# Splitting four output stores at the end of a convolution-and-MLP kernel into halves of 64 rows

## The chip, the cores and the metric

The kernel runs on one core of a Trainium2 chip. The metric is the device time of one execution in microseconds (us); lower is better. Each quoted time of a kernel is the median of several executions.

## The reference

The input is `x` with 8 sequences of 4096 positions and 192 features. Each position is replaced by a weighted sum of itself and the six positions before it (zeros ahead of the start); the seven weights are a softmax, one set for each of eight groups of 24 features. The 32768 resulting rows go through a two-layer perceptron with a leaky ReLU:

```
out[b,s,f] = sum_k softmax(weight)[head(f), k] * x_pad[b, s+k, f]
h = out.reshape(B*S, 192) @ w_in        # 192 -> 2048
g = maximum(0.01*h, h)
result = g @ w_out                      # 2048 -> 192, float32, 32768 rows
```

## The kernel before

**Tiling.** Two sequences are handled side by side, one on partitions 0 to 63 and the other on 64 to 127 (the index `e`), and a block is 512 positions of such a pair. There are 32 blocks. The first two are cut into two groups of 256 positions each, so that the main loop (L654) runs over 34 groups.

**Work in a group.** VectorE computes the convolution of the next group (L226, L232). TensorE multiplies by `w_in` (`mm1`, L494), ScalarE applies the leaky ReLU while it moves the product from PSUM to the tile `g` (L501), and TensorE multiplies an earlier group's `g` by `w_out`. In most of the program this second product is computed transposed (`mm2_slot`, L574); VectorE turns it back (`evac_t`, L596) into the tile `o_t`, and four DMAs on SP's queue (L610) store it, each reading 32 partitions.

**The end.** The last block has no later group to hide behind. Its second product is computed untransposed, in eight pieces of 128 rows (L715 to L719), which I call p0 to p7. In the code they have the numbers `LAST` to `LAST + 7`, where `LAST` is 16. For each piece TensorE runs 16 matmuls of 128x192 (`mm2_one`, L511) into a PSUM tile `po`, and then `evac_o` (L615) is called:

- VectorE copies the `po` tile to an SBUF tile `o_sb` (L622). For these pieces every call takes a new tile (L618, L619).
- SP issues one DMA that stores the 128 rows of 192 floats (L625). That is 96 KB.

**What orders the end.** The pool of `o_sb` tiles has four buffers (L66), so the copies of p4 to p7 write the buffers of p0 to p3 and wait until those stores have landed. The PSUM pool has four buffers too (L68), so the matmuls of p4 wait for the copy of p0, and so on. The program is laid out by hand (L70): SP takes its DMAs in the order of the code. So the stores of p0 to p7 stand behind the four `o_t` stores of the group before.

**Completion semaphores.** The built program gives SP's DMAs eight completion semaphores in rotation. Each DMA waits, before SP issues it, for the DMA that used the same semaphore eight places earlier. I call these semaphores lanes. At the end of the kernel before, the four `o_t` stores of the next-to-last group have lanes 0 to 3, p0 to p3 have lanes 4 to 7, and p4 to p7 have lanes 0 to 3 again.

Of the kernel before, what the change touches and what calls it, by code (L numbers as in the profile page):

```python
# [15 lines left out]
def kernel(  # L16
# [8 lines left out]
    nc = tc.nc  # L25
# [46 lines left out]
    out_rows = out.rearrange("(r s) d -> r s d", r=B)  # L72
# [226 lines left out]
    for sign, off in ((1, 0), (-1, GRP - 1)):  # L299
        nc.gpsimd.affine_select(  # L300
            out=sel[:, :, 0, :], in_=sel[:, :, 0, :], compare_op=mybir.AluOpType.is_ge,
# [42 lines left out]
    for h in range(2):  # L344
        cs = slice(h * NFC // (2 * RUN), (h + 1) * NFC // (2 * RUN))
        nc.gpsimd.dma_start(
            out=w_out.rearrange("p (c i) d -> p c i d", i=RUN)[:, cs],
            in_=moe_w_out.rearrange("(c p i) d -> p c i d", p=128, i=RUN)[:, cs],
# [7 lines left out]
    def warm(n, cols=HT):  # L356
# [10 lines left out]
        out=nmax, in_=w9[:, 0:K], axis=mybir.AxisListType.X,  # L367
# [3 lines left out]
        out=w9[:, 0:K], in_=w9[:, 0:K], func=mybir.ActivationFunctionType.Exp,  # L371
# [61 lines left out]
    for p in range(2):  # L433
# [10 lines left out]
        out=rsum, in0=wml[:, :, K:], scalar=1e-9, in1=whm[:, :, 0, K:],  # L444
# [34 lines left out]
    LAST = len(subs)  # L479
# [39 lines left out]
    def mm2_row_slot(q):  # L519

        p, fc = divmod(q, 2 * NFC)
        rnd, fc = divmod(fc, NFC)
        pair = (2 * p, 2 * p + 1)
        first, last = fc == 0, fc == NFC - 1
        if first and rnd == 0:
            for n in pair:
                po[n] = psum_o.tile([128, D], FP32, name="po", tag="po")
        for rt in range(2):  # L530
            ins = mm2_one(
                rt, pair[rt ^ rnd], fc, first and rnd == 0, last and rnd == 1
            )
            if first and rnd == 1:
                sync(ins, seal, "both row tiles have left these banks")
        if last and rnd == 0:
            seal_round(p, ins)
        if last and rnd == 1:
            evac_o(pair[0])

    def seal_round(p, ins):


        nonlocal seal
        if p == 0:
            seal = nc.scalar.copy(out=junk, in_=junk)
        else:
            seal = evac_o(2 * p - 1)
        sync(seal, ins, "between the rounds")
# [65 lines left out]
    def evac_o(n):  # L615
        b, e, s = subs[n]
        rp, st = divmod(b, NB)
        if n % 2 == 0 or n >= LAST:  # L618
            osb[n] = o_pool.tile([128, 2, D], FP32, name="o_sb")  # L619
        o_sb = osb[n if n >= LAST else n - n % 2]  # L620
        copy = nc.scalar.copy if b < NHALF else nc.vector.tensor_copy
        ins = copy(out=o_sb[:, n % 2, :], in_=po.pop(n))  # L622
        if n >= LAST:
            t0 = st * ST + s * 128
            nc.sync.dma_start(out=out_rows[2 * rp + e, t0 : t0 + 128, :], in_=o_sb[:, n % 2, :])  # L625
        elif n % 2 == 1:
            t0 = st * ST + (s - 1) * 128
            nc.sync.dma_start(
                out=out_rows[2 * rp + e, t0 : t0 + 256, :].rearrange("(c p) d -> p c d", p=128),
                in_=o_sb,  # L630
            )
        return ins
# [21 lines left out]
    for i, grp in enumerate(groups):  # L654
        blk, t0, T = grp
# [10 lines left out]
        for j in range(steps):  # L666
# [41 lines left out]
            if i == NSW and j == steps - 1:  # L708
                evac_o(LAST - 1)
                slot = NSW * NR * NFC  # L710
# [39 lines left out]
```

## Time and profile before

| what | us |
|---|---|
| median of 4 executions | 681.55 |
| their range | 681.27 to 681.7 |
| the profiled execution, whole time | 681.7 |
| its span, first to last instruction | 680.0 |
| outside the span (681.7 - 680.0) | 1.7 |
| TensorE busy | 675.8 |

The profile is of one execution. Its times count from the start of the span. "SPq" rows are DMAs as SP issues them: the duration of such a row is the time that SP is held, not the time in which the data move. The time from issue to landing is given apart, and ends when the completion is seen. A chain of waits follows the work that ended last back to what released it.

### The profile page before, as it was taken

What the parts mean: (1) busy time and instruction counts of PE and PEld (TensorE: products, weight loads), DVE (VectorE), ACT (ScalarE), POOL (GpSimd) and SP (SyncE); (2) the same over time, 40 slices, a digit from 0 to 9 for tenths busy, and PEclk for the clock granted to TensorE, in tenths of its full rate; (3) what the DMA queues carried; (4) which work ended last, traced back from release to release, by engine and by line L of the source; (5) the groups of instructions that cost most, each with busy time, mean ns of one, the idle gap of its engine ahead of it and who ended that gap; (6) DMA issues with size and microseconds to landing.
All of it is one profiled execution on the core that took longest, in us unless ns stands there. A gap on an engine that the chain in (4) does not pass through costs nothing.

```text
span 680.0 us, 27088 instructions
## 1 busy us (share of the span) xinstructions
PE 675.8 (99%) x12444; PEld 447.3 (66%) x12444; DVE 481.5 (71%) x811; ACT 518.7 (76%) x608; POOL 146.3 (22%) x205
## 2 busy tenths in 40 slices
PE   9999999999999999999999999999999999999998
PEld 6997666666666666666666666666666666666667
DVE  7989468766768666778667687667786676876612
ACT  7899777777777778777777877778777777777781
POOL 7455210222201222211222112222022220000000
PEclk9999999999999999999999999999999999999999
DMA  9799846666647557556557476565575573321123
GB/s 153 91 111 110 57 80 88 80 64 73 91 76 96 71 56 89 81 87 86 64 65 94 75 95 77 56 83 83 84 91 66 59 96 71 72 56 35 32 50 94
DMA packets 213826, 53.27 MB, mean 78 GB/s; under 512 B 209232, under 2 KB 213328, under 8 KB 213712
## 3 DMA queue, kind: packets, MB, share of 16 engines
q0 software_dynamic: 98752, 13.97, 30.2%
q1 hardware_dynamic: 114944, 37.57, 27.8%
q8 instruction: 97, 1.59, 0.9%
q14 instruction: 17, 0.14, 0.1%
q10 hardware_dynamic: 16, 0.00, 0.0%
HBM read 28.31 MB, written 25.17 MB: 79 GB/s over the span
## 4 chain that ended last, share of the span: by engine, by line
PE 99%; ACT 0%; DVE 0%; issue 0%
PE ph L494 49%; PE acc L574 44%; PE po L511 5%; PE acc L257 1%; PE warm L358 0%; PE ptr L188 0%; ACT xt L199 0%; PE ptr L179 0%; DVE o_sb L622 0%; PE wps L394 0%
## 5 line engine op out<-in xcount | busy, mean ns | idle before, releaser
L501 ACT ACTIVATE g<-ph 128x1024 bf16<-128x1024 f32 x512 | 496.6, 1021 | 140.5 <-PE ph L494 140.3
L232 DVE SCALAR_TENSOR_TENSOR yt<-xt,wk,yt 128x512 bf16<-128x512 bf16 (+1 forms) x582 | 381.3, 727 | 0.2
L494 PE MATMUL ph<-yt,w_in 64*64 64x512 bf16 (+2 forms) x6048 | 377.1, 369 | 0.0
L574 PE MATMUL acc<-g,w_out 64*64 64x512 bf16 x5568 | 339.9, 376 | 0.0
L494 PEld LDWEIGHTS <-w_in 64*64 64x64 bf16 (+1 forms) x6048 | 229.1, 131 | 103.1 <-issue 0.8
L574 PEld LDWEIGHTS <-w_out 64*64 64x64 bf16 x5568 | 178.6, 118 | 118.7
L99 POOL DMA_DIRECT2D x_bf<-in_x_dram x180 | 133.9, 774 | 409.1 <-DMA xt<-x_bf 407.2
L596 DVE STREAM_TRANSPOSE o_t<-acc 128x512 f32<-128x512 f32 x87 | 73.3, 883 | 181.6 <-PE acc L574 181.6
L511 PE MATMUL po<-w_out,g 64*128 64x192 bf16 (+1 forms) x640 | 36.8, 243 | 0.0
L511 PEld LDWEIGHTS <-g 64*128 64x128 bf16 (+1 forms) x640 | 32.6, 95 | 3.2 <-issue 0.4
L226 DVE TENSOR_SCALAR yt<-xt,wk 128x512 bf16<-128x512 bf16 (+1 forms) x97 | 29.2, 328 | 3.2 <-DMA xt<-x_bf 3.0
L584 ACT COPY junk<-junk 128x1 f32<-128x1 f32 x58 | 11.1, 192 | 4.1
L622 DVE COPY o_sb<-po 128x192 f32<-128x192 f32 x8 | 2.8, 357 | 6.8 <-PE po L511 3.8
L257 PE MATMUL acc<-xt,diag 64*64 64x256 bf16 x140 | 5.4, 272 | 0.2 <-ACT xt L199 0.2
L622 ACT COPY o_sb<-po 128x192 f32<-128x192 f32 x16 | 5.1, 324 | 0.3
L257 PEld LDWEIGHTS <-diag 64*64 64x64 bf16 x140 | 4.4, 106 | 1.2 <-issue 0.7
L358 PE MATMUL warm<-const-bfloat16-1.0 128*128 128x512 bf16 (+3 forms) x12 | 3.9, 477 | 0.8 <-PEq L734 0.8
L152 POOL DMA_DIRECT2D x_half<-in_x_dram x6 | 4.2, 714 | 1.2 <-DMA w_in<-in_moe_w_in_dram 1.2
L358 PEld LDWEIGHTS <-const-bfloat16-1.0 128*128 128x128 bf16 x12 | 1.5, 135 | 2.5 <-issue 2.5
L148 POOL DMA_DIRECT2D x_rows<-in_x_dram x4 | 2.9, 742 | 0.0
L413 DVE TENSOR_TENSOR diag<-ident,whm 128x448 bf16<-128x448 bf16 (+1 forms) x5 | 2.6, 581 | 0.0
L421 ACT ACTIVATE diag<-ident,whm 128x64 bf16<-128x64 bf16 x10 | 2.5, 337 | 0.0
(47 smaller groups left out, 24.6 us busy)
## 6 DMA issues: line engine op xcount, KB each, us to landing
out_dram<-o_t SPq DMA_DIRECT2D x116, 192.0 KB, 4.6
x_bf<-in_x_dram POOLq DMA_DIRECT2D x180, 64.0 KB, 3.1
out_dram<-o_sb SPq DMA_DIRECT2D x8, 192.0 KB, 3.2
xt<-x_bf SPq DMA_TRANSPOSE x90, 3.9
w_out<-in_moe_w_out_dram POOLq DMA_DIRECT2D x2, 384.0 KB, 7.9
out_dram<-o_sb SPq DMA_DIRECT2D x8, 96.0 KB, 2.0
w_in<-in_moe_w_in_dram POOLq DMA_DIRECT2D x2, 256.0 KB, 5.3
x_nat<-in_x_dram SPq DMA_DIRECT2D x2, 192.0 KB, 2.7
```

What stands on the lines that cost most here:

```text
L99: ins = nc.gpsimd.dma_start(out=t[:, c, :, e, :], in_=src[2 * rp + e, :, :, c * CH : (c + 1) * CH],)
L226: lambda s=src, d=dst, c=c: nc.vector.tensor_scalar_mul(d, s, wk[:, c, 0:1])
L232: lambda s=src, d=dst, c=c, k=k: nc.vector.scalar_tensor_tensor(out=d, in0=s, scalar=wk[:, c, k : k + 1], in1=d, op0=mybir.AluOpType.mult, ...
L257: lambda k=k, p=p, a=a, ps=ps, to=to, acc=accs[e * apart]: nc.tensor.matmul(out=acc[to, :T], lhsT=diag[c][ps, p, k, :], rhs=xt[0][ps, c, a ...
L358: nc.tensor.matmul(out=wa[:, 0, 0:cols], lhsT=ones[:, 0:128], rhs=ones[:, 0:cols], start=True, stop=True,)
L494: nc.tensor.matmul(out=ph[m : m + M, e, i * T : (i + 1) * T], lhsT=w_in_of(f, e, c, m, m + M), rhs=y[ps, c, t0 : t0 + T], start=(c == chun ...
L501: act = nc.scalar.activation(out=g[blk][:, nf * u : nf * (u + 1), :, t0 : t0 + T], in_=ph.rearrange("p e (i t) -> p i e t", i=nf), func=my ...
L511: return nc.tensor.matmul(out=po[m], lhsT=g[b][ps, fc, e, s * 128 : (s + 1) * 128], rhs=w_out[ps, fc, :], start=start, stop=stop,)
L574: ins = nc.tensor.matmul(out=acc2[gi, r][e * CH : (e + 1) * CH, 0:T], lhsT=w_out_of(ps, fc, r), rhs=g[b][ps, fc, e, t0 : t0 + T], start=fi ...
L584: seal = nc.scalar.copy(out=junk, in_=junk)
L596: nc.vector.transpose(out=osb[gi, 0][:, 0 : T // GB, :, r], in_=acc2.pop((gi, r))[:, 0:T].rearrange("p (j k) -> p j k", k=GB),)
L622: ins = copy(out=o_sb[:, n % 2, :], in_=po.pop(n))
```

## The change

The stores of p0 to p3 become two DMAs each, one for rows 0 to 63 and one for rows 64 to 127. The stores of p4 to p7 remain one DMA each; this includes the last one. Nothing else differs: the instructions of the four compute engines keep their order, and SP issues 12 DMAs where it issued 8.

```diff
         if n >= LAST:
             t0 = st * ST + s * 128
-            nc.sync.dma_start(out=out_rows[2 * rp + e, t0 : t0 + 128, :], in_=o_sb[:, n % 2, :])
+            parts = 2 if n < LAST + 4 else 1
+            for h in range(parts):
+                ps = slice(h * 128 // parts, (h + 1) * 128 // parts)
+                nc.sync.dma_start(
+                    out=out_rows[2 * rp + e, t0 + ps.start : t0 + ps.stop, :],
+                    in_=o_sb[ps, n % 2, :],
+                )
```

With four more DMAs the lanes move on. The halves of p0 and p1 take lanes 4, 5, 6 and 7, the halves of p2 take 0 and 1, those of p3 take 2 and 3, and p4 to p7 take 4 to 7.

## The prediction, made before the changed kernel ran

> **What bounds the kernel now.** I read the chain of waits first, for the last 20 us. Columns: start, duration, what.
>
> ```profile
> 666.14 10.68 PE po L511 x128
> 676.82 0.02 issue
> 676.85 0.36 DVE o_sb L622
> ```
>
> TensorE runs the eight pieces without a gap until 676.82, and VectorE's copy of p7 follows at once. After 677.21 (676.85 + 0.36) only the store of p7 and its landing remain. So the change, which touches no TensorE work, can act on this tail alone: it must delay the copy or the store of p7 to cost anything, and cannot end TensorE earlier.
>
> Next, VectorE in order of time. A bracket gives the idle time before an instruction and what ended it.
>
> ```profile
> 667.67 0.36 DVE L622 COPY o_sb<-po 128x192 f32<-128x192 f32 x1
> ...
> 671.63 0.36 DVE L622 COPY o_sb<-po 128x192 f32<-128x192 f32 x1 [0.96 <-PE po L511]
> 674.86 1.02 DVE L622 COPY o_sb<-po 128x192 f32<-128x192 f32 x3 [2.87 <-DMA out_dram<-o_sb]
> 676.85 0.36 DVE L622 COPY o_sb<-po 128x192 f32<-128x192 f32 x1 [0.96 <-PE po L511]
> ```
>
> The copies of p0 to p3 follow TensorE. That of p4 waits 2.87 us for the store of p0, whose buffer it needs; those of p5 and p6 run right behind it. The copy of p7 waits for TensorE alone. The stores already hold this row up, but they have caught up by p7.
>
> Third, SP's issues one at a time.
>
> ```profile
> 667.80 0.32 SPq L610 DMA_DIRECT2D out_dram<-o_t  x1
> 668.15 0.49 SPq L610 DMA_DIRECT2D out_dram<-o_t  x1
> 668.69 0.74 SPq L610 DMA_DIRECT2D out_dram<-o_t  x1
> 669.47 1.13 SPq L610 DMA_DIRECT2D out_dram<-o_t  x1
> 670.70 1.08 SPq L625 DMA_DIRECT2D out_dram<-o_sb  x1
> 671.88 1.04 SPq L625 DMA_DIRECT2D out_dram<-o_sb  x1
> 673.01 0.38 SPq L625 DMA_DIRECT2D out_dram<-o_sb  x1
> 673.49 0.38 SPq L625 DMA_DIRECT2D out_dram<-o_sb  x1
> 675.25 0.33 SPq L625 DMA_DIRECT2D out_dram<-o_sb  x1
> 675.67 0.38 SPq L625 DMA_DIRECT2D out_dram<-o_sb  x1
> 676.15 0.40 SPq L625 DMA_DIRECT2D out_dram<-o_sb  x1
> 677.23 0.33 SPq L625 DMA_DIRECT2D out_dram<-o_sb  x1
> ```
>
> The copy of p0 is done at 668.03, but its store is issued at 670.70: SP is busy with the four `o_t` stores, whose issues grow longer as they queue. p0 and p1 are held over 1 us each; from p2 on an issue takes 0.33 to 0.40 us, and two in a row start 0.42 to 0.48 us apart. SP is idle from 673.87 to 675.25 and from 676.55 to 677.23. The times from issue to landing, asked one by one, are 4.0, 3.1, 2.2 and 2.0 us for p0 to p3, 1.7 for p5 and p6, and 1.6 for p7. So p3 lands at about 675.5 (673.49 + 2.0), 1.3 us before its buffer is wanted. Then:
>
> ```profile
> SPq L745 <- DMA out_dram<-o_sb: 1.0, 1, 1.0
> ```
>
> At the end SP waits for the last store. 677.23 + 1.6 = 678.8 is its landing; the span ends 1.2 us later.
>
> **What the Trainium skill says.** Perfetto Trace Analysis, DMA Instruction — HWDGE (DVE, Sync): the shown issue covers waiting for and using the descriptor generator; moving the data is not in it, and the completion comes after the write is confirmed. The trace agrees: p7 is issued in 0.33 us and lands after 1.6. DMA: Bandwidth & Descriptors, Why a DMA increments its semaphore by 16 and not by 1: a transfer uses the largest number of engines up to 16 that divides its outer size, so 64 rows should still use 16. Its Rules for kernel authors call two transfers of partition halves not worth making, since they serialize on the same engines. Nothing in this trace has halves of a store, so neither is shown here yet.
>
> **The change, part by part.**
>
> *Four more issues.* SP's work up to p7 grows by four issues. Their price isn't shown for 64 rows. The nearest row is the freely running 128-row store, one each 0.42 to 0.48 us. If the price went with rows it would be half, so four extra issues cost between 0 (half price each, same total) and 1.9 us (4 x 0.48) of SP. I take 0.47 for each, because an issue of 128 rows takes as long as the first `o_t` store (0.33 and 0.32 us), which moves twice the bytes: it looks like a fixed price.
>
> *The two long issues.* p0 and p1 were held to 671.78 and 672.92. The `o_t` issues end at 669.43 and 670.60, then p0's and p1's 1.18 and 1.14 us on. p0 has half the bytes of an `o_t` store and waits as long as the fourth of them, so I read this as one DMA let through for each `o_t` store that is worked off. If so, the two holds fall on the two halves of p0: issued at 670.70 and 671.88. If instead a hold goes with bytes, two halves take one hold together.
>
> *SP's new timetable.* p1 starts at 673.01, as p2 did. At 0.47 us each, six halves start at 673.01, 673.48, 673.95, 674.42, 674.89 and 675.36; the last is the second half of p3. p4 to p6 follow at 675.83, 676.30 and 676.77, and p7 may start from 677.24, against 677.23 now. So SP's queue itself just fits: the cover is the 1.4 and 0.7 us in which SP was idle. With 0.48 us p7 comes at 677.33.
>
> *Copy of p4.* It needs both halves of p0. The second, issued at 671.88, lands by 675.0 at most (p1's 3.1 us, and p1 had more bytes ahead), so the copy moves from 674.86 to at most 675.2 and ends at 675.5. SP wants it at 675.83: covered, with 0.3 us to spare.
>
> *Copy of p7: the new late one.* It needs the second half of p3. Issued at 675.36, it lands 1.65 us later by the undisturbed stores (1.6 and 1.7); I allow 1.4 (half the data to move, an estimate of mine) to 2.0 (p3's own). The copy of p4 shows 674.86 - (670.70 + 4.0) = 0.16 us from landing to copy. So the copy starts at 675.36 + 1.65 + 0.16 = 677.17 instead of 676.85, the store at 677.55 (0.36 for the copy, 0.02 to the issue), and the end moves by 0.32 us. With the bounds (0.42 us issues and 1.4, 0.48 and 2.0) the copy starts between 676.67, which is hidden behind TensorE, and 677.57: 0 to 0.7 us. Nothing else is queued behind this copy on VectorE, and only SP's last store waits for it.
>
> *Lanes.* The halves of p3 wait for lanes 2 and 3, which the third and fourth `o_t` stores release: 668.69 + 5.2 = 673.9 and 669.47 + 5.0 = 674.5. SP reaches them at 674.89 and 675.36: no cost. All else is older: p4 to p7 take lanes of p0 and p1, landed by about 675.2. The waits at the end cover eight lanes as before.
>
> *Sum.* 0 (TensorE) + 0 (SP's queue) + 0.3 (copy of p7) = 0.3 us: a span of 680.3, whole time 682.0 against the profiled 681.7. That execution is 0.15 us above the median of 681.55, so I predict a median of 681.85.
>
> **The rivals.**
>
> *Hidden altogether.* Issues and holds go with bytes: two halves cost one whole. Then p2 is done at about 673.4, p3's halves wait for their lanes until 673.9 and 674.5, the second lands at about 676.2 (674.5 + 1.7) and TensorE's 676.85 covers it. 681.55. For it: the issues of `o_t` grew as data queued. Against it: p0's hold was no shorter than that of a transfer of twice the size.
>
> *Slower: the hold stays on.* If every half is held as p0 and p1 were, eight halves start 1.13 us apart; the last starts at 670.70 + 7 x 1.13 = 678.6, lands at 680.3, and p7 is stored at 680.3 + 0.16 + 0.38 = 680.8 instead of 677.23: +3.6 us, 685.2. It exceeds 0.2% (1.36 us, about what a measurement of this kernel can tell from no change) once the last half starts after 676.85 + 1.36 - 0.16 - 1.65 = 676.4, an average of 0.81 us for each. Against it: p2 and p3 took 0.38 us with older stores still in flight.
>
> *A gain.* Smaller first stores could free a buffer earlier, but a copy waits for both halves, and p4's copy isn't on the chain. Only run-to-run spread remains, 681.3. That the change does nothing is excluded: the built program shows eight stores of 64 rows ahead of four of 128.
>
> **How the numbers follow.** Forecast (0 to 0.7 us more, most likely 0.3): 0.50. Hidden: 0.37. Hold stays on: 0.10, most of it over 1.36 us. Gain: 0.03. The range takes the first two with the runs' spread of some 0.2 us: 681.35 to 682.45, leaving out the slow rival and half of the gain, under 2 in 10. By sign: faster by over 0.2% 0.02, within 0.2% 0.89, slower 0.09.
>
> **What would show it.** SP: two halves of p0 held about 1.1 us each, then about 0.47 us apiece, p7 issued at about 677.5; a last VectorE copy released by a store and not by TensorE. Hidden: p7's copy still at 676.85. I am wrong if later halves are held over 0.8 us, or a half lands later than a whole.

## The result and the profile after

The changed kernel takes 682.69 us (median of 34 runs, 682.34 to 683.79) against 681.60 for the kernel before (54 runs). The ratio is 1.0017, with a 95% interval of 1.0012 to 1.0022. So the change costs 1.1 us. I had forecast 0.3 us, with 682.45 as the upper end of the range: the sign and the place were right and the size was not.

First, TensorE's last row in the changed kernel, then the end of the chain of waits. Columns: start, duration, what.

```profile
666.18 10.73 PE L511 MATMUL po<-w_out,g 128*128 128x192 bf16 x128
```

```profile
676.15 1.98 DMA out_dram<-o_sb
678.13 0.03 issue
678.16 0.05 DVEq L622
678.21 0.04 issue
678.25 0.36 DVE o_sb L622
```

TensorE ends at 676.91 (666.18 + 10.73). The same row of the kernel before is

```profile
666.07 10.73 PE L511 MATMUL po<-w_out,g 128*128 128x192 bf16 x128
```

It ends at 676.80, so the two clocks differ by 0.11 us here. The chain no longer goes from TensorE to the copy of p7. A store stands between them: the second half of p3, issued at 676.15, lands 1.98 us later, and only then may p7 be copied.

I use one measure from here on: the time from TensorE's end to the issue of p7's store. It was 677.23 - 676.80 = 0.43 us before. It is 678.64 - 676.91 = 1.73 us now, by the last row of SP's issues:

```profile
669.58 1.13 SPq L610 DMA_DIRECT2D out_dram<-o_t  x1
670.81 1.06 SPq L628 DMA_DIRECT2D out_dram<-o_sb  x1
671.92 0.99 SPq L628 DMA_DIRECT2D out_dram<-o_sb  x1
673.01 0.54 SPq L628 DMA_DIRECT2D out_dram<-o_sb  x1
673.60 0.59 SPq L628 DMA_DIRECT2D out_dram<-o_sb  x1
674.29 0.54 SPq L628 DMA_DIRECT2D out_dram<-o_sb  x1
674.88 0.59 SPq L628 DMA_DIRECT2D out_dram<-o_sb  x1
675.57 0.54 SPq L628 DMA_DIRECT2D out_dram<-o_sb  x1
676.15 0.59 SPq L628 DMA_DIRECT2D out_dram<-o_sb  x1
676.85 0.54 SPq L628 DMA_DIRECT2D out_dram<-o_sb  x1
677.49 0.37 SPq L628 DMA_DIRECT2D out_dram<-o_sb  x1
677.95 0.40 SPq L628 DMA_DIRECT2D out_dram<-o_sb  x1
678.64 0.33 SPq L628 DMA_DIRECT2D out_dram<-o_sb  x1
```

The first two halves are held as p0 and p1 were. After that, every issue of a half takes 0.54 or 0.59 us, and a pair of halves comes every 1.28 us (673.01, 674.29, 675.57, 676.85). Before, two whole stores in a row past the holds started at most 0.48 us apart. The first whole store behind the halves (676.85) still takes 0.54, the next ones 0.37 and 0.40. The halves also land late. By the profile's list of DMA issues (size of one, median time to landing), the median half needs 2.0 us, though it moves half of what each of the whole stores p4 to p7 moves:

```profile
out_dram<-o_sb SPq DMA_DIRECT2D x8, 48.0 KB, 2.0
out_dram<-o_sb SPq DMA_DIRECT2D x4, 96.0 KB, 1.7
```

The copies on VectorE:

```profile
674.92 0.36 DVE L622 COPY o_sb<-po 128x192 f32<-128x192 f32 x1 [2.82 <-DMA out_dram<-o_sb]
675.69 0.36 DVE L622 COPY o_sb<-po 128x192 f32<-128x192 f32 x1 [0.41 <-PE po L511]
676.97 0.36 DVE L622 COPY o_sb<-po 128x192 f32<-128x192 f32 x1 [0.92 <-PE po L511]
678.25 0.36 DVE L622 COPY o_sb<-po 128x192 f32<-128x192 f32 x1 [0.92 <-DMA out_dram<-o_sb]
```

From p5 on they come 1.28 us apart, at the pace of the halves. Here the bracket misleads for p5 and p6. TensorE had finished p6 by about 675.6 (seven eighths of 10.73 us after 666.18), while the second half of p2, whose buffer p6 takes, landed at 676.9 (674.88 + 2.0). When a wait names an engine that had long been done, look for a store.

### The profile page after: what moved, and what is told of

Read it like the earlier page. It is cut to its first block, busy times and chain, and to the rows that moved or that the text cites. A ratio compares the mean times of both kernels' runs of the same rounds, so it can differ in the third digit from the quotient of the medians.

```text
span 681.2 us, 27096 instructions
## 1 busy us (share of the span) xinstructions
PE 676.1 (99%) x12444; PEld 447.1 (66%) x12444; DVE 481.5 (71%) x811; ACT 518.8 (76%) x608; POOL 146.0 (21%) x205
## 2 busy tenths in 40 slices
DMA packets 213890, 53.27 MB, mean 78 GB/s; under 512 B 209296, under 2 KB 213392, under 8 KB 213776
## 4 chain that ended last, share of the span: by engine, by line
PE 98%; DMA 1%; SPq 0%; DVE 0%; issue 0%; DVEq 0%
PE ph L494 49%; PE acc L574 44%; PE po L511 4%; PE acc L257 1%; DMA out_dram<-o_sb 1%; PE warm L358 1%; SPq L628 0%; DVE o_sb L622 0%; PE ptr L188 0%; PE ptr L179 0%; PE warm L394 0%; DVEq L622 0%; PE wps L394 0%
```

## The experiments

My theory at this point was that the forecast's mechanism holds, but that a half costs SP 0.64 us and lands in 2.0. Open were whether SP's queue, the buffer wait or something shared carries the cost, and why a half is dearer than a whole. Each edit is against the changed kernel. A median is of 12 to 34 runs, but of two for 32 + 64 + 32 rows, four for four of 32 and five for 64 x 96. The last column is the measure above, from the one trace of each kernel.

| stores of p0 to p3 | median us | before, run beside it | ratio and interval | p7 after TensorE, us |
|---|---|---|---|---|
| whole (kernel before) | 681.60 | | | 0.43 |
| two halves (changed kernel) | 682.69 | 681.60 | 1.0017 (1.0012 to 1.0022) | 1.73 |
| second halves on ScalarE's queue | 681.47 | 681.60 | 0.9998 (0.9989 to 1.0006) | 0.43 |
| two column halves | 681.36 | 681.60 | 0.9998 (0.9990 to 1.0006) | 0.49 |
| only p3 in halves | 681.50 | 681.60 | 0.9998 (0.9989 to 1.0006) | 0.43 |
| halves, own buffers | 682.67 | 681.76 | 1.0015 (1.0008 to 1.0021) | 1.43 |
| 32 + 64 + 32 rows | 684.82 | 681.76 | 1.0048 (1.0029 to 1.0066) | 3.31 |
| even and odd rows | 682.58 | 681.76 | 1.0013 (1.0007 to 1.0020) | 1.78 |
| p0 to p2 in halves | 681.92 | 681.76 | 1.0005 (0.9996 to 1.0013) | 1.02 |
| 96 + 32 rows | 681.59 | 681.58 | 1.0000 (0.9991 to 1.0009) | 0.43 |
| four of 32 rows | 685.22 | 681.58 | 1.0052 (1.0037 to 1.0067) | 3.97 |
| 80 + 48 rows | 681.31 | 681.72 | 0.9993 (0.9985 to 1.0002) | 0.50 |
| p0, p1 in four of 64 x 96 | 683.86 | 681.72 | 1.0032 (1.0019 to 1.0045) | 2.78 |

### The second halves on another queue

```diff
-                nc.sync.dma_start(
+                (nc.scalar if h else nc.sync).dma_start(
```

> The changed kernel, with the second half of each split store issued by ScalarE's queue, which is idle at the end. Theory (the price is SP's issue time): SP has eight issues again and p7's copy starts at TensorE's end; 681.6 us, as the kernel before. Rival (what is slow is something that both queues share[...]): SP's issues stay about 0.6 us apart, and the kernel stays 0.5 to 1.1 us slower than before.

SP's halves of p2 and p3, and the store of p7:

```profile
673.80 0.47 SPq L628 DMA_DIRECT2D out_dram<-o_sb  x1
674.76 0.47 SPq L628 DMA_DIRECT2D out_dram<-o_sb  x1
677.54 0.33 SPq L628 DMA_DIRECT2D out_dram<-o_sb  x1
```

The cost is gone: p7 is issued 677.54 - (666.38 + 10.73) = 0.43 us after TensorE, as before. ScalarE issued its four halves as soon as each copy was done, the first at 668.37. So what delays the kernel is the time that SP needs to issue all the halves in its one queue.

The two halves shown take 0.47 us, less than the 0.54 of a first half in the changed kernel. SP stood idle just before each (0.33 and 0.49 us), until the DMA that had the same lane, here one of ScalarE's, had landed. A whole store after such a pause takes 0.33 to 0.36, so the half is the dearer one here too. The queues do share something: the lanes are one example, and the first half on SP was held for 1.37 us, more than the 1.06 of the changed kernel.

### Only the last of the four

```diff
-            parts = 2 if n < LAST + 4 else 1
+            parts = 2 if n == LAST + 3 else 1
```

> Only the store of p3 is split into halves of 64 rows; p0 to p2 stay whole. Theory (the cost is the sum of issues that no longer fits in SP's idle time): the second half of p3 starts at about 674.1, lands before 676.4, and nothing on the chain moves: 681.6 us, as the kernel before. Rival (a split store in the buffer's way costs by itself, by landing later or by holding p4): p7's copy moves and the kernel is 0.3 us or more slower.

SP's third whole store, the two halves of p3, and p4:

```profile
673.39 0.38 SPq L628 DMA_DIRECT2D out_dram<-o_sb  x1
673.87 0.56 SPq L628 DMA_DIRECT2D out_dram<-o_sb  x1
674.48 0.58 SPq L628 DMA_DIRECT2D out_dram<-o_sb  x1
675.54 0.34 SPq L628 DMA_DIRECT2D out_dram<-o_sb  x1
```

The theory holds. The dear issues are there (0.56 and 0.58), the first of them straight behind a whole store, but SP's idle time before p4 takes them in and the time is that of before. A half's price is its own; it needn't stand behind other halves.

### Three of four

```diff
-            parts = 2 if n < LAST + 4 else 1
+            parts = 2 if n < LAST + 3 else 1
```

> Only p0, p1 and p2 are split into halves; p3 is stored whole. Theory (SP's timetable with 0.64 us for each half after the two long holds): p3 is issued at about 675.5 on the clock of the kernel before, lands 1.75 us later, and p7's copy starts at 677.4 instead of 676.85: 0.5 us slower than before (682.1), p7 issued 1.0 us after TensorE's end. Rival (it is p3's own split, whose second half lands late, that costs): no cost, 681.6.

The store of p3, and the copy of p7 that waits for it:

```profile
675.61 0.53 SPq L628 DMA_DIRECT2D out_dram<-o_sb  x1
```

```profile
677.57 0.36 DVE L622 COPY o_sb<-po 128x192 f32<-128x192 f32 x1 [0.19 <-DMA out_dram<-o_sb]
```

p7 is issued 677.95 - (666.20 + 10.73) = 1.02 us after TensorE, as worked out, though p3 itself is whole. The rival, that p3's own split is the cost, falls. The times alone don't settle it: the interval of 0.9996 to 1.0013 (-0.3 to +0.9 us) holds both +0.5 and nothing.

### Buffers of their own

```diff
+    tail_pool = ctx.enter_context(tc.tile_pool(name="tail", bufs=8))
...
-            osb[n] = o_pool.tile([128, 2, D], FP32, name="o_sb")
+            osb[n] = o_pool.tile([128, 2, D], FP32, name="o_sb") if n < LAST else tail_pool.tile([128, 1, D], FP32, name="o_one")
...
```

Eight more tiles of the old size would take 12 KB of each partition, and 10.7 KB are free, so the new ones hold one piece each and not two. The lines left out adapt the copy and the store to that.

> The changed kernel, with eight output tiles of their own (one for each of the last pieces), so that no copy waits for a store. Measure: from the end of TensorE's last matmul to the issue of p7's store, 0.4 us in the kernel before and 1.7 us in the changed one. Theory (two limits one behind the other: SP's queue, and the copy of p7 that waits for the second half of p3): SP's first nine issues stay where they are, p7 is issued right behind p6 at 1.5 us, and the kernel is some 0.2 us faster than the changed one, still 0.9 us slower than before (682.5). Rival (the wait for the buffer is all of it): 0.4 us again, 681.6 us.

```profile
677.12 0.36 DVE L624 COPY o_one<-po 128x192 f32<-128x192 f32 x1 [0.96 <-PE po L512]
```

```profile
676.91 0.53 SPq L630 DMA_DIRECT2D out_dram<-o_one  x1
677.55 0.38 SPq L630 DMA_DIRECT2D out_dram<-o_one  x1
678.01 0.40 SPq L630 DMA_DIRECT2D out_dram<-o_one  x1
678.51 0.40 SPq L630 DMA_DIRECT2D out_dram<-o_one  x1
```

Now p7 is copied as soon as TensorE is done with it (677.12), but its store waits for SP until 678.51, directly behind p6: 1.43 us after TensorE against 1.73. So there are two limits one behind the other. The buffer wait adds 0.3 us; SP's queue alone accounts for the other 1.0. That split is read from the two traces; the medians (682.67 and 682.69) don't show the 0.3. Taking the buffer wait away would have been the wrong cure.

### Columns instead of rows

```diff
-                ps = slice(h * 128 // parts, (h + 1) * 128 // parts)
+                cs = slice(h * D // parts, (h + 1) * D // parts)
                 nc.sync.dma_start(
-                    out=out_rows[2 * rp + e, t0 + ps.start : t0 + ps.stop, :],
-                    in_=o_sb[ps, n % 2, :],
+                    out=out_rows[2 * rp + e, t0 : t0 + 128, cs],
+                    in_=o_sb[:, n % 2, cs],
```

> The changed kernel, with each of the four stores split by columns (two DMAs of 128 rows x 96 columns) instead of by rows. Theory (64 rows are a dear shape to issue): issues come every 0.47 us as whole stores do, the second half of p3 starts at about 675.4, and the kernel is 0.3 us slower than before (681.9). Rival (any four more DMAs cost that, whatever their shape): issues stay 0.64 us apart and the kernel is 1.1 us slower than before (682.7).

The two parts of p3 and the store of p4:

```profile
674.61 0.38 SPq L628 DMA_DIRECT2D out_dram<-o_sb  x1
675.03 0.43 SPq L628 DMA_DIRECT2D out_dram<-o_sb  x1
675.56 0.38 SPq L628 DMA_DIRECT2D out_dram<-o_sb  x1
```

The same four extra DMAs, with the same 48 KB each, now cost nothing that the times can tell, where I had expected 0.3 us. A pair takes 0.95 us (674.61 to 675.56) instead of 1.28, and those of p2 and p3 land in 1.6. That is about the timetable of the forecast, whose pair took 0.94; p7 comes after 0.49 us, where the forecast had 0.75 (677.55 - 676.80). So not the number of DMAs but the shape is dear.

### Which property of the shape: the place

```diff
-                ps = slice(h * 128 // parts, (h + 1) * 128 // parts)
                 nc.sync.dma_start(
-                    out=out_rows[2 * rp + e, t0 + ps.start : t0 + ps.stop, :],
-                    in_=o_sb[ps, n % 2, :],
+                    out=out_rows[2 * rp + e, t0 + h : t0 + 128 : parts, :],
+                    in_=o_sb[h::parts, n % 2, :],
```

> The changed kernel, with each of the four stores split into even and odd rows instead of upper and lower: 64 partitions each, spread over the whole memory. Theory A (the place of the 64 partitions): issues 0.47 us apart, landing 1.6 us, and 681.6 to 681.9 us. Rival B (the number of rows): issues 0.64 us apart, landing 2.0, 682.7 us as the changed kernel.

The second part of p2 and the two of p3:

```profile
674.84 0.59 SPq L627 DMA_DIRECT2D out_dram<-o_sb  x1
675.53 0.55 SPq L627 DMA_DIRECT2D out_dram<-o_sb  x1
676.12 0.59 SPq L627 DMA_DIRECT2D out_dram<-o_sb  x1
```

Spread over the whole memory, 64 rows are as dear to issue. The theory of the place falls for the issue price. It holds for a small part. In the trace's packets (one row of 768 bytes each), the median row of an upper or lower half takes 51 ns, and the 64 rows of a half 0.37 us. With even and odd rows they take 35 ns and 0.28 us; a row of a whole store takes 36 ns. The Trainium skill, SBUF — State Buffer, Door 1: The DMA port swizzle, says that 64 neighbouring partitions from 0 or from 64 reach only half of the memory's 16 ports; the packets agree. But landing only moves from about 2.0 to 1.9 us, and no time is won.

The same with three parts:

```diff
-            parts = 2 if n < LAST + 4 else 1
+            parts = 3 if n < LAST + 4 else 1
...
-                ps = slice(h * 128 // parts, (h + 1) * 128 // parts)
+                ps = slice(0, 128) if parts == 1 else slice((0, 32, 96)[h], (32, 96, 128)[h])
```

> The stores of p0 to p3 are cut into three: rows 0 to 31, 32 to 95 and 96 to 127. It is slower than the changed kernel in any case (four more issues); what counts is each issue and the data behind it. Theory A (a half is slow because its 64 neighbouring partitions, all in the lower or all in the upper half of the memory, share fewer paths): the middle 64 rows, which lie in both halves, are issued in about 0.4 us and land in 1.6, as a whole does, and the 32 rows are as slow as a half or slower. Rival B (fewer than 128 rows are slow, wherever they lie): the middle is issued in 0.54 to 0.59 us and lands in 2.0, like the halves.

The three parts of p1:

```profile
674.19 0.35 SPq L628 DMA_DIRECT2D out_dram<-o_sb  x1
674.58 0.52 SPq L628 DMA_DIRECT2D out_dram<-o_sb  x1
675.14 0.58 SPq L628 DMA_DIRECT2D out_dram<-o_sb  x1
```

Both were wrong in part. The middle's issue takes 0.52 us and it lands in 1.8, near the rival's figures, although its packets take 35 ns. The 32 rows ahead of it take 0.35 to 0.37, and those behind it 0.57 or 0.58. So there is a cost that comes with the 64 rows and falls partly on the DMA after them, while 32 rows by themselves are cheap. That was the hint.

### Which property of the shape: the count of rows

```diff
-                ps = slice(h * 128 // parts, (h + 1) * 128 // parts)
+                ps = slice(0, 128) if parts == 1 else slice((0, 96)[h], (96, 128)[h])
```

> The stores of p0 to p3 are cut into 96 and 32 rows. Open is what makes a 64-row store dear. Theory S (64 rows are a dear count in themselves): an issue after the two long holds takes about 0.38 us, as with whole stores and columns, p3's second part lands at about TensorE's end, and p7 is issued 0.4 to 0.9 us after TensorE's end (681.6 to 682.1). Rival F (any count of rows below 128 is dear, except the short tail of 32): the 96 rows are issued and followed as the 64 are, 0.54 to 0.59 us, and p7 comes 1.4 us or more after TensorE's end (682.6 or more).

```diff
-            parts = 2 if n < LAST + 4 else 1
+            parts = 4 if n < LAST + 4 else 1
```

> The stores of p0 to p3 are cut into four of 32 rows, so that SP issues 20 DMAs. Theory S (64 rows are dear in themselves): 32 rows take 0.36 to 0.40 us each, 14 of them after the two holds some 6 us, and p7 is issued about 3.5 us after TensorE's end (684.7). Rival F (fewer rows are dearer): 0.55 us or more each, p7 issued 6 us after TensorE's end (687).

With 96 + 32, the issues behind the two long holds take 0.36 to 0.43 us and p7 comes after 0.43. With four of 32, each takes 0.36 to 0.43 too. That kernel is slow for their number, eight more than in the changed kernel: fourteen of them stand behind the two holds, 0.47 us apart. p7 comes after 3.97 us, 0.5 later than I had expected.

A cut close to halves, with the same edit but 80 and 48 rows:

> The stores of p0 to p3 are cut into 80 and 48 rows, nearer to halves than 96 and 32. Theory S (64 rows alone are dear): issues of 0.37 to 0.43 us as with 96 and 32, p7 issued 0.4 to 0.6 us after TensorE's end, 681.6 us. Rival (two parts of about half the rows are dear): 0.54 to 0.59 us and 1.7 us, 682.7.

The two parts of p3 and the store of p4:

```profile
674.57 0.37 SPq L628 DMA_DIRECT2D out_dram<-o_sb  x1
674.98 0.42 SPq L628 DMA_DIRECT2D out_dram<-o_sb  x1
675.50 0.37 SPq L628 DMA_DIRECT2D out_dram<-o_sb  x1
```

Cheap again, p7 after 0.50 us. Finally, 64 rows with half the length, for p0 and p1 only:

```diff
-            parts = 2 if n < LAST + 4 else 1
+            parts = 4 if n < LAST + 2 else 1
...
-                ps = slice(h * 128 // parts, (h + 1) * 128 // parts)
+                ps = slice(0, 128) if parts == 1 else slice(h // 2 * 64, (h // 2 + 1) * 64)
+                cs = slice(0, D) if parts == 1 else slice(h % 2 * 96, (h % 2 + 1) * 96)
...
-                    out=out_rows[2 * rp + e, t0 + ps.start : t0 + ps.stop, :],
-                    in_=o_sb[ps, n % 2, :],
+                    out=out_rows[2 * rp + e, t0 + ps.start : t0 + ps.stop, cs],
+                    in_=o_sb[ps, n % 2, cs],
```

> Only p0 and p1 are cut, each into four parts of 64 rows x 96 columns, so that SP issues 14 DMAs. Theory S (the 64 rows count, whatever their length): 0.54 to 0.59 us each after the two holds, p7 issued about 2.7 us after TensorE's end. Rival (it is the combination of 64 rows with 768 bytes each): 0.38 to 0.43 us each, about 1.5 us after TensorE's end.

Three parts in a row, all of p1:

```profile
674.43 0.59 SPq L629 DMA_DIRECT2D out_dram<-o_sb  x1
675.07 0.59 SPq L629 DMA_DIRECT2D out_dram<-o_sb  x1
675.71 0.59 SPq L629 DMA_DIRECT2D out_dram<-o_sb  x1
```

Dear again, 0.64 us apart, and p7 after 2.78 us. So of the other counts tried (32, 48, 80, 96 and 128 rows) none costs SP over 0.43 us once the long holds are past, except straight behind 64 rows. 64 rows cost 0.52 to 0.60 in a series and 0.47 after a pause, with rows of 384 or 768 bytes, upper, lower, middle or alternate. Why SP needs more for this count is open; no view shows what it does inside an issue.

None of the variants is clearly faster than the kernel before. That fits: p7's store already followed TensorE by 0.43 us, of which 0.36 are its copy.

## Why the prediction was wrong

- **What bounds the kernel: right.** TensorE's end, then p7's copy, store and landing. TensorE's row is 10.73 us long in both kernels.
- **The two long holds fall on the two halves of p0: right.** On the clock of before (0.11 us earlier) the first half of p1 starts at 672.90; I had 673.01. In every variant on SP's queue alone the first two DMAs behind the `o_t` stores were held, for 0.87 to 1.14 us, whether of 96 KB or of 24. So the holds go with the number of DMAs and not with bytes. That one is let through for each `o_t` store worked off is not shown by this.
- **"I take 0.47 for each, because an issue of 128 rows takes as long as the first `o_t` store": the step that failed.** The argument was that the price doesn't depend on the shape, so a half costs as much as a whole. I bounded it by 0 and by 0.48 and so left out that half a store can cost more than a whole one. It costs 0.64 us on average (1.28 for two), and no other number of rows that was tried had that price by itself. The second half of p3 was to start 1.44 us ahead of TensorE's end (676.80 - 675.36) and started 0.76 ahead (676.91 - 676.15): 0.68 us late.
- **Landing in 1.65 us, at most 2.0: at its upper bound.** It took 1.98, 0.33 us more than I took. "Half the data to move" pointed the wrong way. Most of it is the dear issue again, since the time to landing includes the issue: counted from the end of the issue, this half needed 1.39 us (1.98 - 0.59) and the whole store of p6 1.3 (1.7 - 0.40). A half that lands later than a whole was one of my signs of being wrong, and it came true.
- **The sum.** Forecast shift of p7's copy 0.32; with 0.68 and 0.33 added and 0.04 off (0.12 us from landing to copy, not 0.16) 1.29 us. The trace has 678.25 - 676.91 = 1.34 against 676.85 - 676.80 = 0.05, which is the same 1.29. The medians differ by 1.1.
- **SP's queue "just fits": wrong for the same reason.** With buffers of their own, the queue alone still cost 1.0 us.
- **Lanes and the copy of p4: right, no cost.** The copy of p4 is at 674.92, 674.81 on the clock of before; I had allowed 675.2.
- **The slow rival** was right that later halves are dear, but not in the cause. It was to cost over 1.36 us from an average of 0.81 us for each of seven halves; measured were (676.15 - 670.81) / 7 = 0.76, a little under that, and 1.1 us. The holds did not stay on: they ended where I had put their end, and each later half took 0.54 or 0.59.
- **The skill's remarks.** 16 engines for 64 rows (DMA: Bandwidth & Descriptors, Why a DMA increments its semaphore by 16 and not by 1) agrees with the packet count. By that page each engine that takes part adds one write to the semaphore; there are 64 packets more, 213890 against 213826, which is 16 for each of four more DMAs. The advice in the page's Rules for kernel authors against two transfers of partition halves held here. But the page gives the shared engines as the reason, and what cost here was the issue.

## What to carry to other kernels

Before splitting a transfer, add up what the issuing queue has to do until the last transfer that matters, against its idle time there, and price the new shape from a row of just that shape; without one, allow for a part that costs more than the whole. A buffer that is reused after a store puts that store's issue and landing on the path of the last piece. When a split near the end is wanted, splitting by columns, into two unequal parts of the rows or over a second queue cost nothing here that the times can tell (intervals up to 1.0009), where halves of 64 rows cost 1.1 us.

## What the runs showed of the hardware that I had not expected

- A store of 64 rows takes SP 0.52 to 0.60 us to issue in a series past the long holds, and one of 32, 48, 80, 96 or 128 rows 0.35 to 0.43. After a pause it is 0.47 for 64 rows and 0.33 to 0.36 for 128. What stands right behind 64 rows is dear too: 0.53 or 0.54 for a whole store, 0.57 or 0.58 for 32 rows.
- Past the holds, a 64-row store of 48 KB lands 1.8 to 2.0 us after its issue starts, a whole one of 96 KB after 1.6 to 1.7 (1.8 right behind 64 rows), and one of 32 rows (24 KB) after 1.5 (1.7 right behind 64 rows).
- Rows from 64 neighbouring partitions in one half of the memory move at a median of 51 ns each, those from 64 alternate partitions at 35.
